# Attention and two MLPs on one core: the MLP's tiles moved to multiples of 512 bytes, and new numbers in the list scheduler

## The chip, the cores and the metric

One core of a Trainium2 chip runs the whole program. The metric is device time in microseconds (us) of one execution. Engines are called as in the profile: PE is TensorE's matmul, PEld its weight load (both are issued by one sequencer), DVE is VectorE, ACT is ScalarE, POOL is GpSimd, SP issues the DMAs.

## What is computed

```
def phi(x):                                   # w_phi: 64 x 128
    proj = x @ w_phi
    proj = proj - max(abs(proj), axis=-1)
    return concat([exp(proj), exp(-proj)])
kv = phi(k).T @ v ; z = sum(phi(k))           # 4 batches, 8 heads, 576 tokens, head 64
attn = (phi(q) @ kv) / (phi(q) @ z + 1e-6)
x = attn                                      # 2304 tokens x 512
h = x @ w_in ; g = where(h > 0, h, exp(min(h, 0)) - 1) ; x = g @ w_out      # MLP 1, 2048 wide
h = x @ w_in2 ; g = h * clip(h + 3, 0, 6) / 6 ; out = g @ w_out2            # MLP 2, 2048 wide
```

The weights of both MLPs arrive as 64-bit floats, everything else in 32 bits.

## The kernel before

**Attention.** Eight units (two heads of two batches each) go through projections, exponentials, the product with v and the normalization. Their result is written into one resident tile `x32` (512 features in four slices of 128 partitions, 2304 tokens).

**MLPs.** Every matmul operand is a pair of fp32r tiles, the rounded value (hi) and the rest (lo), and every product is three matmuls: hi by hi, lo by hi, hi by lo. The hidden width of 2048 is worked in 8 groups of 256 per MLP, `g` from 0 to 15 over both (`NP` = 8). The 2304 tokens are five blocks, four of 512 and one of 256 (block 4). Blocks 0 and 1 are pair `pr` 0, blocks 2 and 3 are pair 1. For a pair, `x @ w_in` of a group is done with seven products P1 to P7 instead of eight (`hid`, L710; Winograd's form of Strassen's scheme), on sums and differences of the quarters: of x they are called A11, A12, A22, S1 to S4, of w_in B11, B21, B12, B22, T1 to T4. Such a product is 6 matmuls of 512 columns. For block 4 it is done directly (`hid4`, L724, twice 12 matmuls of 256 columns). The product with w_out is `outp` (L775): 6 matmuls per block and slice, of 512 columns (256 for block 4 of MLP 1). In a matmul one operand is stationary (loaded by LDWEIGHTS, 128 columns) and one moves. In L710 and L724 w_in is stationary and x moves. In L775 the hidden tile (`ga` or `gb`) moves and w_out is stationary in MLP 1; in MLP 2 it is the other way round.

**Around the matmuls.** The operands of x are made by `x_add` (L687, sums in place), `x_hi` (L693 on ACT, L660 on POOL) and `x_lo` (L696, on DVE for A11, A22, S1, S2 and on POOL for A12, S3, S4). A hidden bank gets its activation by `act1` (ACT, L744 to L747), `gate` (DVE, L751), `gate_hi` (ACT, L755) and `gate_lo` (DVE, L758), and a bank of `x @ w_in` is free again after `gate_lo`; `snap` (ACT, L732) and `join` (DVE, L737) add up the seven products. `sums` (DVE, L787) adds a bank of `outp` to `x32`; three banks serve `outp`, so its next-but-two use waits for that addition. A weight comes by DMA and is turned into fp32 by `low` (ACT), `size` and `end` (POOL, L635 and L651), `sign` and `up` (DVE); then `part_hi` (L664) and `part_lo` (L668) make the hi and lo of w_in, `out_hi` (L673) and `out_lo` (L677) those of w_out. There are 8 w_in tiles, one group's worth, and 3 of w_out.

**Order.** The order of PE's work in the MLPs is written out by hand. Between the MLPs (`g` = 8) it is P1 and P2 of pair 0, the last four `outp` of block 4 of MLP 1 (`kept`), P6, P7, P5, the first `hid4`, P3, P4, the second `hid4`, and then P1 of pair 1. All other engines are ordered by a list scheduler, `in_order`: every step has a duration, the steps that it waits for, and a rank; of the steps of an engine that could start within 0.3 us the one with the lowest rank goes first. The ranks are due times: an operand of x is due `PREP` before its use (16 and 18 us for the two MLPs), the conversions of w_in `W_IN_LEAD` before the group's first product, those of w_out `W_OUT_LEAD` before the first `outp`; steps on hidden banks are due when their product ends. Durations and ranks decide the order in the program alone, not what waits for what.

**Layout.** Tiles are stacked from both ends of a partition's memory. On the left stand `x32`, two small constants, an unused tile `gap`, then `wp` (w_in, w_out), `stg` (staging), and the operands of x but for three; on the right stand, from the end of memory down, S2 and S4 of pair 0, block 4 of x (`x_b4`), `ma`, `mb`, `ga` and `gb`. Each of these tiles is a multiple of 512 bytes, so all tiles of a side share one remainder.

Of the kernel before, what the change touches and what calls it, by code (L numbers as in the profile page):

```python
# [29 lines left out]
}  # L30
KVT = 0.118
W_LEAST, W_MOST = 2.0 ** -15, 122879.9921875
W_IN_LEAD, W_OUT_LEAD = 30.0, 25.0
PREP = (16.0, 18.0)


class Token:
# [111 lines left out]
def attention_then_two_mlps(  # L149
# [67 lines left out]
    nc.gpsimd.memset(half_c, 0.5)  # L217
    two_c = const.tile([128, 1], F32, name="two_c")
    nc.gpsimd.memset(two_c, 2.0)
    const.tile([128, 124], F32, name="gap")  # L220

    wp = ctx.enter_context(tc.tile_pool(name="wp", bufs=1))
    stg = ctx.enter_context(tc.tile_pool(name="stg", bufs=1))
# [586 lines left out]
    def on(engine, us, fn, rank, after):  # L810
        name, us = ("POOL", us[1]) if engine is nc.gpsimd else ("ACT" if engine is nc.scalar else "DVE", us[0])
        return step(name, us, fn, after=after, rank=rank, port=name == "DVE")

    def split(m, pr, op, kk, at, deps, e_hi, e_lo):
        home = last_use[pr, op] if m else [OPEN["b" if pr == 1 else "e" if pr == 0 and op in EARLY else "a"]]
        rank = need[m, pr, op] - PREP[m]
        size = BLOCKS[at[0]][1] / 512
        hi = on(e_hi, (0.05 + 0.52 * size, 0.1 + 0.56 * size), bind_(x_hi, e_hi, pr, op, kk, at), rank, deps + home)
        lo = on(e_lo, (0.1 + 0.6 * size, 0.1 + 1.3 * size), bind_(x_lo, e_lo, pr, op, kk, at), rank, [hi])
        readers.setdefault(at, []).extend([hi, lo])  # L820
        ready.setdefault((m, pr, op), []).append(lo)
        return [hi, lo]
# [89 lines left out]
    def convert(key, lead):  # L912
        m, w, i, c = key
        ts_, ta, tb = Token("s"), Token("ca"), Token(("bi", "bo")[i])
        x = step("SP", 1.4, bind_(fetch, *key), takes=[ts_], rank=lead - 5, behind=[chain[0]] if chain[0] else [])
        chain[0] = x
        low, size, sign, up, end = to_f32(key)
        x = step("ACT", 0.85, low, after=[x], rank=lead, takes=[ta, tb], uses=[ts_])
        z = step("DVE", 0.5, sign, after=[x], rank=lead, port=True, uses=[ts_])
        x = step("POOL", 0.45, size, after=[x], rank=lead)  # L920
        x = step("DVE", 0.3, up, after=[x], rank=lead, port=True)
        return step("POOL", 0.75, end, after=[x, z], rank=lead, uses=[ta, tb]), tb

    for g in range(2 * NP):
        m, w = g // NP, 2 * (g % NP)
        lead = first[g] - W_IN_LEAD
        keys = {"B11": (m, w, 0, 0), "B21": (m, w, 0, 1), "B12": (m, w + 1, 0, 0), "B22": (m, w + 1, 0, 1)}
        done, tok, raw_ = {}, {}, {}

        def part(name, key, after, users):  # L930
            t = wi_tok[g, name] = Token("wi")
            hi = step("ACT", 0.36, bind_(part_hi, g, name, key), after=after, rank=lead, takes=[t], uses=users,
                      behind=[chain[1]] if chain[1] else [])
            chain[1] = hi
            lo = step("POOL", 0.75, bind_(part_lo, g, name, key), after=[hi], rank=lead, uses=users + [t])
# [12 lines left out]
        t3 = differ("B12", "B22", "B12", [done["B12"], raw_["B22"], t1])
        t2 = differ("B22", "B22", "B11", [done["B22"], t1, t3])
        t4 = differ("B21", "B21", "B22", [done["B21"], t2])  # L950
        part("T2", keys["B22"], [t2], [tok["B22"]])
        part("T3", keys["B12"], [t3], [tok["B12"]])
        part("T1", keys["B11"], [t1], [tok["B11"]])
        part("T4", keys["B21"], [t4], [tok["B21"]])
        lead = first_o[g] - W_OUT_LEAD
        for fi in range(2):
            t = wo_tok[g, fi] = Token("wo")
            for c in range(2):
                x, tb = convert((m, w + fi, 1, c), lead)
                hi = step("ACT", 0.36, bind_(out_hi, m, w + fi, c), after=[x] + ([OUT[g, fi]] if c else []),  # L960
                          rank=lead, takes=[] if c else [t], uses=[tb])
                OUT[g, fi] = step("POOL", 0.75, bind_(out_lo, m, w + fi, c), after=[hi], rank=lead, uses=[tb, t])

# [27 lines left out]

    clock = BEGIN
# [7 lines left out]
    for x in order:  # L1000
# [53 lines left out]
        else:  # L1054
# [45 lines left out]
def bind_(fn, *a):  # L1100
    return lambda: fn(*a)
# [50 lines left out]
```

## Time and profile before

| | |
|---|---|
| time, median of 3 runs | 952.58 us (951.78 to 953.23) |
| the profiled execution: its time, its span | 952.91 us, 950.8 us |
| attention, until the first matmul of an MLP | 157.9 us |
| PE busy | 918.8 us, 97% of the span |
| DVE, ACT, POOL busy | 676.0, 566.6, 399.7 us |

The span runs from the first to the last instruction that the profiler saw; the other 2.1 us lie around it. PE is busy nearly all the time, but a matmul's duration in the trace overlaps with the next one, so what a matmul costs PE is the distance from its start to the start of the next.

### The profile page before, as it was taken

To read this page: it belongs to the slowest core of one execution; us is meant where nothing else is said; L and a number is where in the kernel's file an instruction comes from. 1 tells how busy PE (TensorE), PEld (TensorE's weight loads), DVE (VectorE), ACT (ScalarE), POOL (GpSimd) and SP (SyncE) were. 2 spreads that over 40 slices of the span, in tenths; PEclk is the share of its full clock that TensorE was granted. 3 is DMA by queue.
4 is the path that set the end of the run, shared out by engine and by line. 5 is a ranking of instruction groups with operands and counts; after the bars stand their busy time and mean duration, and the time that the engine had idled before them with its cause. 6 is when DMAs were issued, how large, how long until landed. Compare 5 with 4: busy or idle time off the path is not lost.

```text
span 950.8 us, 17635 instructions
## 1 busy us (share of the span) xinstructions
PE 918.8 (97%) x6792; PEld 762.3 (80%) x6792; DVE 676.0 (71%) x1202; ACT 566.6 (60%) x1207; POOL 399.7 (42%) x570
## 2 busy tenths in 40 slices
PE   8999999899999999999999968999999999999998
PEld 7888787688888888888878856888888888888886
DVE  6888877855676767676767797467767676777555
ACT  5686766876665656565666755665545454545331
POOL 0258621453544444444442646545444444444200
PEclk9999999999999999999999987999999999999999
DMA  8534510001111111111111001111111111010013
GB/s 228 160 110 124 147 47 2 1 27 41 45 45 45 45 46 45 45 44 46 45 42 43 29 22 36 43 56 55 46 56 34 57 34 56 33 56 23 1 67 133
DMA packets 42532, 53.69 MB, mean 56 GB/s; under 512 B 21328, under 2 KB 21456, under 8 KB 42448
## 3 DMA queue, kind: packets, MB, share of 16 engines
q1 hardware_dynamic: 42448, 52.57, 17.8%
q8 instruction: 53, 0.87, 0.4%
q14 instruction: 31, 0.25, 0.1%
HBM read 47.84 MB, written 4.72 MB: 55 GB/s over the span
## 4 chain that ended last, share of the span: by engine, by line
PE 88%; DVE 6%; ACT 5%; issue 1%; POOL 0%; POOLq 0%; ACTq 0%
PE ps_a L775 27%; PE ps_p L710 25%; PE ps_t L775 13%; PE ps_t L710 6%; PE ps_t L430 4%; PE ps_a L380 4%; PE ps_p L724 3%; PE ps_p L318 3%; ACT e L407 2%; DVE x L687 1%; DVE x_S L696 1%; PE ps_t L452 1%; PE ps_t L724 1%; DVE x L787 1%; DVE x_A L696 1%
## 5 line engine op out<-in xcount | busy, mean ns | idle before, releaser
L710 PE MATMUL ps_p<-x_S,w_in 128*128 128x512 f32 x630 | 162.6, 397 | 10.0 <-POOL x_S L696 4.1
L787 DVE TENSOR_TENSOR x<-ps_a,x 128x512 f32<-128x512 f32 (+1 forms) x177 | 116.4, 660 | 50.4 <-PE ps_a L775 49.0
L710 PEld LDWEIGHTS ps_p<-x_S,w_in 128*128 128x128 f32 x630 | 118.4, 189 | 39.4 <-POOL x_S L696 4.9
L710 PE MATMUL ps_p<-x_A,w_in 128*128 128x512 f32 x468 | 120.9, 399 | 3.4 <-DVE ga L758 3.4
L668 POOL TENSOR_TENSOR w_in<-w_bi,w_in 128x256 fp32r<-128x256 f32 x128 | 97.7, 782 | 44.7 <-ACT w_in L664 44.2
L635 POOL TENSOR_SCALAR w_a<-w_a 128x256 f32<-128x256 f32 x128 | 53.9, 422 | 146.5 <-ACT w_a L630 146.1
L710 PEld LDWEIGHTS ps_p<-x_A,w_in 128*128 128x128 f32 x468 | 88.5, 191 | 23.3 <-DVE ga L758 4.2
L787 DVE TENSOR_TENSOR x<-ps_t,x 128x512 f32<-128x512 f32 (+1 forms) x89 | 59.0, 663 | 43.0 <-PE ps_t L775 42.6
L651 POOL TENSOR_TENSOR w_bi<-w_bi,w_a 128x256 int32<-128x256 int32 x64 | 47.9, 757 | 95.0 <-DVE w_a L647 95.0
L677 POOL TENSOR_TENSOR w_out<-w_bo,w_out 128x256 fp32r<-128x256 f32 x64 | 48.1, 751 | 94.3 <-ACT w_out L673 93.6
L775 PE MATMUL ps_a<-w_out,gb 128*128 128x512 f32 x336 | 84.9, 395 | 0.0
L775 PE MATMUL ps_a<-gb,w_out 128*128 128x512 f32 (+1 forms) x384 | 83.2, 358 | 0.6 <-DVE x L787 0.6
L651 POOL TENSOR_TENSOR w_bo<-w_bo,w_a 128x256 int32<-128x256 int32 x64 | 48.3, 756 | 65.0 <-DVE w_a L647 62.3
L775 PEld LDWEIGHTS ps_a<-gb,w_out 128*128 128x128 f32 x384 | 64.8, 188 | 13.2 <-DVE x L787 0.8
L775 PEld LDWEIGHTS ps_a<-w_out,gb 128*128 128x128 f32 x336 | 63.0, 188 | 15.1 <-ACT x L785 0.2
L751 DVE SCALAR_TENSOR_TENSOR ps_p<-ma,ps_p 128x512 f32<-128x512 f32 x66 | 45.8, 693 | 30.8 <-ACT ma L747 16.4
L775 PE MATMUL ps_a<-ga,w_out 128*128 128x512 f32 x258 | 65.6, 395 | 0.5 <-DVE ga L758 0.5
L732 ACT COPY mb<-ps_p 128x512 f32<-128x512 f32 x54 | 31.7, 587 | 57.1 <-PE ps_p L710 56.9
L328 DVE TENSOR_REDUCE mx<-ps_p 128x4 f32<-128x512 f32 (+1 forms) x80 | 50.3, 629 | 15.7 <-PE ps_p L318 15.4
L775 PE MATMUL ps_a<-w_out,ga 128*128 128x512 f32 x240 | 60.1, 397 | 0.0
L775 PEld LDWEIGHTS ps_a<-ga,w_out 128*128 128x128 f32 x258 | 47.6, 188 | 11.6 <-DVE ga L758 0.9
L630 ACT ACTIVATE w_a<-w 128x256 f32<-128x256 f32 x128 | 54.3, 424 | 1.1 <-POOL w_bo L651 1.1
(109 smaller groups left out, 1907.1 us busy)
## 6 DMA issues: line engine op xcount, KB each, us to landing
w<-in_moe_w_in_dram SPq DMA_DIRECT2D x64, 256.0 KB, 2.6
w<-in_moe_w_out_dram SPq DMA_DIRECT2D x64, 256.0 KB, 2.6
vb<-in_v_dram SPq DMA_DIRECT2D x16, 288.0 KB, 4.2
out_dram<-x SPq DMA_DIRECT2D x18, 256.0 KB, 2.0
raw_k<-in_k_dram SPq DMA_DIRECT2D x7, 576.0 KB, 4.5
raw_q<-in_q_dram SPq DMA_DIRECT2D x7, 576.0 KB, 4.9
raw_k<-in_k_dram SPq DMA_DIRECT2D x1, 320.0 KB, 4.9
raw_q<-in_q_dram SPq DMA_DIRECT2D x1, 320.0 KB, 5.3
```

Of the source, the lines that this page charges most:

```text
L328: V.tensor_reduce(out=mx[:, :n], in_=P[j, h], axis=AX.X, op=ALU.max, apply_absolute_value=True)
L380: nc.tensor.matmul(out=acc[bb][f0:f0 + 64, h, half], lhsT=kp[p, i, half, f0:f0 + 64], rhs=vb[u % 2][p, r, h], start=(done.count(bb) == 1 a ...
L430: nc.tensor.matmul(out=ps[p, i, h], lhsT=E[h, c][:, half, r - 4 * c, p], rhs=ST[0][:, bb, h, half], start=(half == 0), stop=(half == 1),)
L630: nc.scalar.activation(out=st["a"], in_=s.bitcast(F32).rearrange("p (n t) -> p n t", t=2)[:, :, 1], func=AF.Abs)
L635: nc.gpsimd.tensor_scalar(out=st["a"], in0=st["a"], scalar1=W_MOST, scalar2=W_LEAST, op0=ALU.min, op1=ALU.max)
L651: nc.gpsimd.tensor_tensor(out=b_, in0=b_, in1=st["a"].bitcast(I32), op=ALU.add)
L668: nc.gpsimd.tensor_tensor(out=t[:, 1], in0=F[key], in1=t[:, 0].bitcast(F32), op=ALU.subtract)
L677: nc.gpsimd.tensor_tensor(out=t[:, 1], in0=F.pop((m, w, 1, c)), in1=t[:, 0].bitcast(F32), op=ALU.subtract)
L710: nc.tensor.matmul(out=PS[ps_], lhsT=t[:, a_, kk], rhs=X[pr, op][x_][kk], start=(opens and i == 0), stop=(i == 5), skip_group_check=True,)
L751: V.scalar_tensor_tensor(out=PS[ps_], in0=MAIN[key], scalar=s, in1=PS[ps_], op0=o0, op1=o1)
L775: nc.tensor.matmul(out=o, lhsT=a_, rhs=b_, start=(fi + j == 0), stop=(fi == 1 and j == 2))
L787: V.tensor_tensor(out=part, in0=ps, in1=part, op=ALU.add)
```

## The change

The unused tile `gap` grows from 496 to 832 bytes, and an unused tile of 480 bytes is put at the end of memory on the right. What stands on the left ahead of `gap` ends at byte 38592. Before, `gap` brings that to 39088, which is rounded up to 39104: 192 bytes over a multiple of 512, and so stand all MLP tiles of the left. On the right the stack ended at byte 229344, and all its MLP tiles stand 480 over a multiple. After, the left begins at 38592 + 832 = 39424 and the right ends at 229344 - 480 = 228864, both multiples of 512. In the matmuls of an MLP every slice of a tile begins at a multiple of 512 bytes in its tile, so a remainder holds for every operand: before, both operands stand at 192 in L710 but for S2 and S4 of pair 0 (480 and 192), and one at 480 and one at 192 in L724 and L775; after, all stand at 0.

In the scheduler `W_IN_LEAD` goes from 30 to 15 us, `PREP` of MLP 2 from 18 to 22 us, and the durations of twelve kinds of steps change by up to 12%, that of `act1` in MLP 2 by 21%. No step is added or removed. Line numbers from L221 on are one higher in the changed kernel.

```
-W_IN_LEAD, W_OUT_LEAD = 30.0, 25.0
-PREP = (16.0, 18.0)
+W_IN_LEAD, W_OUT_LEAD = 15.0, 25.0
+PREP = (16.0, 22.0)
...
-    const.tile([128, 124], F32, name="gap")
+    const.tile([128, 208], F32, name="gap")
+    ctx.enter_context(tc.tile_pool(name="gap", bufs=1, side="right")).tile([128, 120], F32, name="gap_r")
...
-        x = step("ACT", 0.57 * (1 + (m == 0)), bind_(act1, m, key, ps_, ring), after=after + [OPEN["a"]], rank=when,
+        x = step("ACT", 1.23 if m == 0 else 0.69, bind_(act1, m, key, ps_, ring), after=after + [OPEN["a"]], rank=when,
```

On PE the order of the MLPs' matmuls is the same word for word; some steps of attention's units 5 to 7 change places. In a group in the middle of an MLP, ACT, DVE and POOL have some conversions a few places later. The largest moves are between the MLPs, where the operands of x for `g` = 8 now rank 4 us earlier.

DVE there, before, from the `x_lo` of S1's first half on (`x32` is written by `x_add` in L687 and by `sums` in L787; gb_6765 is the hidden tile of block 4 that the last four `outp` of MLP 1 read):

```order
L696 TENSOR_TENSOR x_S1_0_119<-x32_63,x_S1_0_119 128x512
L787 TENSOR_TENSOR x32_63<-ps_a1_6733,x32_63 128x512
L696 TENSOR_TENSOR x_S2_0_2919<-x32_63,x_S2_0_2919 128x512
L758 TENSOR_TENSOR gb_6765<-ps_p1_6609,gb_6765 128x512
L687 TENSOR_TENSOR x32_63<-x32_63 128x512
L696 TENSOR_TENSOR x_A22_0_118<-x32_63,x_A22_0_118 128x512
L787 TENSOR_TENSOR x32_63<-ps_t0_6747,x32_63 128x512
```

The same place after, where gb_6776 is that hidden tile and the first row is the second row behind the first `x_lo` of S2:

```order
L697 TENSOR_TENSOR x_A22_0_122<-x32_63,x_A22_0_122 128x512
L788 TENSOR_TENSOR x32_63<-ps_t0_6700,x32_63 128x512
L688 TENSOR_TENSOR x32_63<-x32_63 128x512
L788 TENSOR_TENSOR x32_63<-ps_a0_6712,x32_63 128x512
L688 TENSOR_TENSOR x32_63<-x32_63 128x512
L788 TENSOR_TENSOR x32_63<-ps_a1_6723,x32_63 128x512
L688 TENSOR_TENSOR x32_63<-x32_63 128x512
L697 TENSOR_TENSOR x_S1_0_123<-x32_63,x_S1_0_123 128x512
L788 TENSOR_TENSOR x32_63<-ps_t0_6735,x32_63 128x512
L697 TENSOR_TENSOR x_S2_0_2923<-x32_63,x_S2_0_2923 128x512
L688 TENSOR_TENSOR x32_63<-x32_63 128x512
L759 TENSOR_TENSOR gb_6776<-ps_p1_6611,gb_6776 128x512
```

The `gate_lo` stood right behind the first `x_lo` of S2 and now stands 13 places behind it, behind the second halves of A22, S1 and S2 too. Ahead of it nine steps are new and three (of a weight's conversion) are gone.

POOL between the MLPs, before (w_out_6831 is the second w_out tile of `g` = 8):

```order
L651 TENSOR_TENSOR w_bo_6579<-w_bo_6579,w_a_6578 128x256
L696 TENSOR_TENSOR x_S3_0_120<-x32_63,x_S3_0_120 128x512
L677 TENSOR_TENSOR w_out_6831<-w_bo_6579,w_out_6831 128x256
L651 TENSOR_TENSOR w_bo_6642<-w_bo_6642,w_a_6641 128x256
L677 TENSOR_TENSOR w_out_6831<-w_bo_6642,w_out_6831 128x256
L696 TENSOR_TENSOR x_S4_0_2920<-x32_63,x_S4_0_2920 128x512 x2
```

and after:

```order
L697 TENSOR_TENSOR x_S3_0_124<-x32_63,x_S3_0_124 128x512
L669 TENSOR_TENSOR w_in_6753<-w_bi_6354,w_in_6753 128x256
L669 TENSOR_TENSOR w_in_6765<-w_bi_6328,w_in_6765 128x256
L669 TENSOR_TENSOR w_in_6768<-w_bi_6252,w_in_6768 128x256
L669 TENSOR_TENSOR w_in_6774<-w_bi_6277,w_in_6774 128x256
L697 TENSOR_TENSOR x_S4_0_2924<-x32_63,x_S4_0_2924 128x512 x2
L678 TENSOR_TENSOR w_out_6542<-w_bo_6480,w_out_6542 128x256
```

The two `x_lo` of S4 stood behind an `end` and the last `out_lo` of the second w_out tile, and now stand ahead of both.

ACT between the MLPs, before, after the `gate_hi` of P5 and P7's bank (ma_6939 and ga_6958 are `act1` and `gate_hi` of P3's bank):

```order
L693 CAST x_S3_1_3111<-x32_63 128x512
L693 CAST x_S2_1_3110<-x32_63 128x512
L693 CAST x_S1_1_3112<-x32_63 128x512
L747 ACTIVATE ma_6939<-ps_p2_6758,half_c_69 128x512
L693 CAST x_S3_1_3111<-x32_63 128x512
L755 CAST ga_6958<-ps_p2_6758 128x512
```

and after, where ma_6930 and ga_6941 are those two, ma_6937 is `act1` of the second `hid4`, gb_6925 is `gate_hi` of a bank that `join` made with P7, and mb_6853 is `act1` of the bank of P7 and P4:

```order
L756 CAST gb_6925<-ps_p1_6886 128x512
L748 ACTIVATE ma_6930<-ps_p2_6745,half_c_69 128x512
L694 CAST x_S3_1_3115<-x32_63 128x512
L748 ACTIVATE ma_6937<-ps_p0_6872,half_c_69 128x512
L756 CAST ga_6941<-ps_p2_6745 128x512
L748 ACTIVATE mb_6853<-ps_t1_6844,half_c_69 128x512
```

The `act1` of P3's bank is now ahead of the `x_hi` of S1 and S2 for pair 1, and its `gate_hi` has the `act1` of the second `hid4` ahead of it.

## Rows read from the trace of the kernel before

**Rows 1.** The page: span, and busy time, share and instructions.

```profile
span 950.8 us, 17635 instructions
PE 918.8 (97%) x6792; PEld 762.3 (80%) x6792; DVE 676.0 (71%) x1202; ACT 566.6 (60%) x1207; POOL 399.7 (42%) x570
```

**Rows 2.** PE's timeline in MLP 1: start, length, line, tiles, count.

```profile
360.29 1.56 PE L775 MATMUL ps_t<-gb,w_out 128*128 128x512 f32 x6
361.69 1.56 PE L710 MATMUL ps_p<-x_S,w_in 128*128 128x512 f32 x6
363.09 2.96 PE L775 MATMUL ps_a<-gb,w_out 128*128 128x512 f32 x12
365.89 1.55 PE L710 MATMUL ps_p<-x_S,w_in 128*128 128x512 f32 x6
367.27 1.52 PE L710 MATMUL ps_t<-x_S,w_in 128*128 128x512 f32 x6
368.63 1.52 PE L710 MATMUL ps_p<-x_A,w_in 128*128 128x512 f32 x6
369.99 1.56 PE L710 MATMUL ps_p<-x_S,w_in 128*128 128x512 f32 x6
```

**Rows 3.** PE's timeline in MLP 2.

```profile
749.54 1.56 PE L724 MATMUL ps_p<-x_b,w_in 128*128 128x256 f32 x12
750.94 2.96 PE L775 MATMUL ps_a<-w_out,ga 128*128 128x512 f32 x12
753.74 1.56 PE L775 MATMUL ps_t<-w_out,ga 128*128 128x512 f32 x6
```

**Rows 4.** Matmuls (PE) and loads of L710, L724, L775, in this order, over both MLPs.

```profile
150.00:951.00 801.00, 340.86 (x1344) 254.67 (x1344) 0.99 0.13 43
150.00:951.00 801.00, 51.02 (x384) 49.57 (x384) 0.99 0.13 43
150.00:951.00 801.00, 431.24 (x1824) 329.07 (x1824) 0.99 0.13 43
```

**Rows 5.** Two stretches: length; PE, PEld, DVE, ACT, POOL busy; granted clock; DMA.

```profile
300.00:350.00 50.00, 50.00 (x245) 41.55 (x245) 35.32 (x64) 30.84 (x66) 21.10 (x33) 1.00 0.13 43
555.00:560.00 5.00, 3.14 (x7) 2.33 (x8) 5.00 (x12) 2.60 (x7) 2.70 (x2) 0.72 0.00 0
```

**Rows 6.** PE's timeline between the MLPs; in brackets idle time and what ended it.

```profile
552.29 0.97 PE L775 MATMUL ps_a<-gb,w_out 128*128 128x256 f32 x6 [0.56 <-DVE x L787]
...
555.72 0.50 PE L710 MATMUL ps_p<-x_S,w_in 128*128 128x512 f32 x1 [1.76 <-ACT x_S L693]
557.36 1.22 PE L710 MATMUL ps_p<-x_S,w_in 128*128 128x512 f32 x2 [1.14 <-DVE x_S L696]
...
568.07 2.64 PE L710 MATMUL ps_p<-x_S,w_in 128*128 128x512 f32 x5 [4.08 <-POOL x_S L696]
570.51 2.76 PE L710 MATMUL ps_t<-x_A,w_in 128*128 128x512 f32 x6
573.07 2.13 PE L724 MATMUL ps_p<-x_b,w_in 128*128 128x256 f32 x12
578.59 5.49 PE L710 MATMUL ps_p<-x_A,w_in 128*128 128x512 f32 x12 [3.39 <-DVE ga L758]
```

**Rows 7.** DVE's timeline between the MLPs.

```profile
546.80 1.18 DVE L696 TENSOR_TENSOR x_S<-x,x_S 128x512 fp32r<-128x512 f32 x1
547.91 0.68 DVE L758 TENSOR_TENSOR gb<-ps_p,gb 128x512 fp32r<-128x512 f32 x1
```

**Rows 8.** POOL's timeline between the MLPs.

```profile
565.34 1.01 POOL L677 TENSOR_TENSOR w_out<-w_bo,w_out 128x256 fp32r<-128x256 f32 x1 [4.17 <-ACT w_out L673]
566.31 3.12 POOL L696 TENSOR_TENSOR x_S<-x,x_S 128x512 fp32r<-128x512 f32 x2
```

**Rows 9.** ACT's timeline between the MLPs.

```profile
574.20 0.62 ACT L693 CAST x_S<-x 128x512 fp32r<-128x512 f32 x1 [6.66 <-DVE x L687]
574.73 0.68 ACT L747 ACTIVATE ma<-ps_p,half_c 128x512 f32<-128x512 f32 x1
576.17 0.59 ACT L755 CAST ga<-ps_p 128x512 fp32r<-128x512 f32 x1 [0.26 <-DVE ps_p L751]
```

More of the change, by code (lines that the diff above doesn't have):

```diff
@@ L817, in split @@
         size = BLOCKS[at[0]][1] / 512
-        hi = on(e_hi, (0.05 + 0.52 * size, 0.1 + 0.56 * size), bind_(x_hi, e_hi, pr, op, kk, at), rank, deps + home)
+        hi = on(e_hi, (0.05 + 0.55 * size, 0.1 + 0.56 * size), bind_(x_hi, e_hi, pr, op, kk, at), rank, deps + home)
         lo = on(e_lo, (0.1 + 0.6 * size, 0.1 + 1.3 * size), bind_(x_lo, e_lo, pr, op, kk, at), rank, [hi])
@@ L917, in convert @@
         low, size, sign, up, end = to_f32(key)
-        x = step("ACT", 0.85, low, after=[x], rank=lead, takes=[ta, tb], uses=[ts_])
-        z = step("DVE", 0.5, sign, after=[x], rank=lead, port=True, uses=[ts_])
+        x = step("ACT", 0.95, low, after=[x], rank=lead, takes=[ta, tb], uses=[ts_])
+        z = step("DVE", 0.45, sign, after=[x], rank=lead, port=True, uses=[ts_])
         x = step("POOL", 0.45, size, after=[x], rank=lead)
@@ L931, in part @@
             t = wi_tok[g, name] = Token("wi")
-            hi = step("ACT", 0.36, bind_(part_hi, g, name, key), after=after, rank=lead, takes=[t], uses=users,
+            hi = step("ACT", 0.40, bind_(part_hi, g, name, key), after=after, rank=lead, takes=[t], uses=users,
                       behind=[chain[1]] if chain[1] else [])
@@ L959, in attention_then_two_mlps @@
                 x, tb = convert((m, w + fi, 1, c), lead)
-                hi = step("ACT", 0.36, bind_(out_hi, m, w + fi, c), after=[x] + ([OUT[g, fi]] if c else []),
+                hi = step("ACT", 0.40, bind_(out_hi, m, w + fi, c), after=[x] + ([OUT[g, fi]] if c else []),
                           rank=lead, takes=[] if c else [t], uses=[tb])
@@ L971, in finish @@
         pt, mt = ptok[ps_], mtok[key]
-        x = step("ACT", 0.57 * (1 + (m == 0)), bind_(act1, m, key, ps_, ring), after=after + [OPEN["a"]], rank=when,
+        x = step("ACT", 1.23 if m == 0 else 0.69, bind_(act1, m, key, ps_, ring), after=after + [OPEN["a"]], rank=when,
                  takes=[mt] if ring else [], uses=[pt, mt])
-        x = step("DVE", 0.64, bind_(gate, m, key, ps_), after=[x], rank=when, uses=[pt, mt])
-        x = step("ACT", 0.57, bind_(gate_hi, key, ps_, tg.ring), after=[x], rank=when, takes=[tg], uses=[tg, pt],
+        x = step("DVE", 0.69, bind_(gate, m, key, ps_), after=[x], rank=when, uses=[pt, mt])
+        x = step("ACT", 0.58, bind_(gate_hi, key, ps_, tg.ring), after=[x], rank=when, takes=[tg], uses=[tg, pt],
                  behind=[gg_last[tg.ring]] if tg.ring in gg_last else [])
         gg_last[tg.ring] = x
-        tiles[key] = step("DVE", 0.65, bind_(gate_lo, key, ps_), after=[x], rank=when, uses=[tg, pt])
+        tiles[key] = step("DVE", 0.685, bind_(gate_lo, key, ps_), after=[x], rank=when, uses=[tg, pt])
     def save(g, pr, key, ring, after, when):
         t = mtok[key] = Token(ring)
-        return step("ACT", 0.57, bind_(snap, (g, pr, "X"), key, ring), after=after, rank=when, takes=[t],
+        return step("ACT", 0.59, bind_(snap, (g, pr, "X"), key, ring), after=after, rank=when, takes=[t],
                     uses=[ptok[g, pr, "X"], t])
@@ L988, in joined @@
             ptok[g, pr, to] = Token("h")
-        return step("DVE", 0.65, bind_(join, (g, pr, bank_), key, (g, pr, to)), after=after, rank=when,
+        return step("DVE", 0.70, bind_(join, (g, pr, bank_), key, (g, pr, to)), after=after, rank=when,
                     takes=[ptok[g, pr, to]] if to != bank_ else [], uses=[pt, ptok[g, pr, to], mtok[key]])
@@ L1074, in attention_then_two_mlps @@
             else:
-                y = step("DVE", 0.65 if m or b < 4 else 0.38, bind_(sums, m, False, b, d), after=[s, adds[m, b, d]], rank=when, uses=[ty])
+                y = step("DVE", 0.66 if m or b < 4 else 0.41, bind_(sums, m, False, b, d), after=[s, adds[m, b, d]], rank=when, uses=[ty])
             adds[m, b, d] = y
```

## The prediction

> **What bounds the kernel now.** I read the page first: PE is busy 918.8 of 950.8 us [rows 1]. That is no proof that matmuls set the time, so I looked at stretches: in the middle of MLP 1 PE is busy 50.00 of 50 us at clock 1.00, and DVE, ACT and POOL 35, 31 and 21 us [rows 5]. No other engine is near its limit there, and PE's timeline shows no wait; the reader is to see in [rows 2] that each group of six follows the one before at once. So the time of the MLPs is a sum of distances from one matmul's start to the next one's, and busy times don't give them, since durations overlap: a group of six has a length of 1.52 to 1.56 us but starts 1.36 to 1.40 us before the next.
>
> These distances are not all alike. With one operand at remainder 480 and the other at 192, six matmuls of 512 columns take 1.40 us: 361.69 to 363.09 in L710 (by PE's order the S2 of pair 0), and in L775 two groups from 363.09 to 365.89 [rows 2]; it is the same in MLP 2, where w_out moves: twelve in 2.80 [rows 3]. With both at 192 they take 367.27 to 368.63 = 1.36 us, and again 1.36, and 1.38 (365.89 to 367.27) where the group ahead was a mixed one [rows 2]. Shape, type and line (L710) are the same; I found no other difference than the addresses. Twelve of 256 columns with mixed remainders take 749.54 to 750.94 = 1.40 [rows 3]. One matmul of 512 is thus 233.3 ns mixed and 226.7 ns equal. At the lower clock six take 570.51 to 573.07 = 2.56 us, 427 ns each [rows 6]; half of it, 213.3 ns, is what 512 columns would take at the higher clock (2.4 instead of 1.2 GHz) without any excess. The excess now is 20 ns or 13.3 ns.
>
> The one place where PE waits long is between the MLPs, 545 to 590 us. Its waits there are 0.56, 1.76, 1.14, 4.08 and 3.39 us, 10.9 in all [rows 6]. Matmuls behind them run at the lower clock for a while; from the groups' distances there, against those of [rows 2], I work out a loss of some 7.9 us in three stretches of 1.9, 3.1 and 3.0 us.
>
> **The addresses.** 3552 matmuls belong to the MLPs [rows 4]. L710 has 1344; of these S2 and S4 of pair 0 are mixed, 2 products x 16 groups x 6 = 192, and 1152 are equal. L775 has 1824, of which block 4 in MLP 1 (8 groups x 4 slices x 6 = 192) has 256 columns, so 1632 have 512. L724 has 384 of 256 columns. All are mixed in L724 and L775. After, every operand stands at 0, so both are equal. No row shows two operands at 0. From above the price is bounded by the mixed 1.40 us, from below by the excess-free 1.28; the nearest row is that of two equal remainders, 1.36, which I take.
>
> - Mixed, 512 columns: 1632 + 192 = 1824, 304 groups of six, each 1.40 - 1.36 = 0.04 shorter: 12.2 us.
> - Equal, 512 columns: 192 groups. In PE's order 126 of them follow a mixed one and lose 0.02 by it: 2.5 us.
> - 256 columns: 384 + 192 = 576, 48 groups of twelve, 0.04 each if the excess falls in the same ratio: 1.9 us.
>
> Together 16.6 us. About 3% of the matmuls lie between the MLPs, where waits or the lower clock decide, so 16 us stay. This rests on PE alone: none of it is covered by other work, since PE waits for nothing, and the other engines keep a margin (DVE 35.32 of 50 [rows 5]); with six in 1.36 a group of the hidden width is 2% shorter, which they can follow.
>
> The Trainium skill ("TensorE: Matmul & The Clock Gate", section "Back-to-back issue gap") gives N/2.4 GHz and some 2.5 ns from start to start, 215.7 ns for 512 columns, whatever the addresses. The rows have 226.7 and 233.3, so the rule does not describe this kernel as it is; if it did after the change, the address term would be about 52 instead of 16.6, by its figure an estimate. The case has its place among the rivals.
>
> **The scheduler in the middle of an MLP.** `W_IN_LEAD` and the durations move some conversions a few places on ACT, DVE and POOL. No instruction is added; a w_in tile is still loaded and converted a group ahead, since the ring has one group's worth, and PE waits nowhere in these stretches. I price it at 0. The cover is PE's own work in a group, some 47 us; what is left idle on the fullest engine, DVE, is 14.7 of 50 us [rows 5]. If the cover failed, the price would be one wait per group of a conversion's length, about 1 us (an `out_lo` took 1.01 [rows 8]) x 16 = 16 us. Attention's units 5 to 7 change places without a change of work: 0, I allow 2 us either way.
>
> **Between the MLPs.** POOL first. PE waits 4.08 us for the `x_lo` of S4 [rows 6], which POOL starts at 566.31, behind an `out_lo` that itself waited 4.17 us for ACT [rows 8]. After, both `x_lo` of S4 stand ahead of it. POOL would have been free before that wait, so S4 comes at least 3 us earlier, and with it P3: 4.08 us goes, together with most of one stretch at the lower clock (3 us).
>
> DVE next. It is full there (5.00 of 5.00 us, while the clock is 0.72 [rows 5]), so an order can only shift the loss. The `gate_lo` of block 4 ran at 547.91 right behind an `x_lo` [rows 7]; now nine steps are new ahead of it and three gone. Nine at 0.68 are 6.1 us, less some 1.4 for the three and 1.25 that DVE idled ahead: about 3.5 us later, so it ends at 552.1 instead of 548.6. The last four `outp` of MLP 1 want it at about 549.2: a new wait of 2.9 us. Queued behind it on PE are P6, P7 and P5. But the second halves of S1 and S2 stand ahead of that `gate_lo` now, so the waits of 1.76 and 1.14 us for S2 [rows 6] go, as does most of the 0.56: 3.4 against 2.9. The next thing to be late would be the `sums` of these `outp` and behind them block 4's operand, which the first `hid4` reads.
>
> ACT last. The 3.39 us ahead of P1 of pair 1 [rows 6] ends with the `gate_lo` of P3's bank. ACT had waited 6.66 us at an `x_hi` with the bank's `act1` queued behind it [rows 9]. After, that `act1` goes ahead, but the `gate_hi` stands behind the `act1` of the second `hid4`, which PE finishes last: `act1`, `gate_hi` and `gate_lo` of 0.68 + 0.59 + 0.68 and some 0.25 of handing over come after it, 2.2 us instead of 3.39: 1.2 saved. Operands of pair 1 that are late on DVE can cost 1.5 to 5 us a little later; I take 3.
>
> Sum: -4.1 - 3.0 - 3.4 + 2.9 - 1.2 + 3 = -5.8, say -6 us. Bounds: all waits and all loss of the clock gone, -10.9 - 7.9 = -19; nothing gone and both new waits added, 2.9 + 3.3 = +6.
>
> **Sum.** The profiled execution took 952.91 us (950.8 and 2.1 around it [rows 1]), 0.3 above the median of the runs. 952.9 - 16 - 6 = 930.9; I say 930 us for the median.
>
> **Rivals.**
>
> *The excess goes away altogether* (0.18). The excess grows with columns and changes with the remainder, so it may come from starting off a boundary, and a multiple of 512 could leave little of it. For: 192 and 480 are both off 512, and no row shows an operand that is on it. Against: one remainder of 192 and one of 480 differ by a third of the excess only. At 1.28 us per group: 304 x 0.12 + 126 x 0.10 + 66 x 0.08 + 48 x 0.12 = 60 us, 58 without the middle: 889 us. Halfway to the equal rows, 1.32, gives some 909. The figure of the skill above would give about 897, an estimate.
>
> *Addresses don't matter* (0.20). The difference could belong to something that goes with the remainder, such as which pools are read, and the change moves all of them. Then the schedule alone remains: 952.9 - 6 = 947 us. Against it: the S2 at 361.69 and the S3 at 367.27 are one line with weights from one pool and differ in nothing else. The Trainium skill ("SBUF — State Buffer", section "Who interferes with whom") says that PE never waits on anyone and has ports of its own for the moving operand and for the weight load; by that the 1.36 and 1.40 of [rows 2] should be one number, and they are not.
>
> *Zero is a bad remainder* (0.08), and the kernel gets slower. Two operands on the same multiple may collide at every start. The groups now sum to 304 x 1.40 + 126 x 1.38 + 66 x 1.36 + 48 x 1.40 = 756 us over 544 groups, 1.391 each; with 6 us from the schedule it decides from 1.402 per group on. One more step of 0.04 above the mixed ones, 1.44, would cost 544 x 0.05 = 27 us: 974 us. Against: of the rows, equal is the faster.
>
> *Schedule and addresses cancel* (0.04): 1.39 per group and +2 between the MLPs, 953 to 955 us.
>
> **Numbers.** The forecast, six in 1.36 everywhere, has 0.50, and its own range from the bounds between the MLPs and in attention is 920 to 941. The range over all, 895 to 949, reaches to most of the case without excess and to the schedule alone, and leaves out the slower ones and the lowest end. A measurement of this kernel can tell about 0.2% (1.9 us) from no change; by that, faster 0.86, same 0.05, slower 0.09.
>
> **What would show it.** Right: every group of six, L710 or L775, in both MLPs starts 1.36 us ahead of the next, twelve of 256 columns in 1.36; no wait of 4.08 us for S4 on POOL; a new wait for `gb` at about 549 us less what the matmuls have gained by then. Wrong in size: groups of 1.28 to 1.34. Wrong in kind: groups still of two lengths, or at 1.40 and more; waits of PE in the middle of an MLP for w_in or for a bank; or a sum of waits between the MLPs above 11 us.

## The result and the profile after

The changed kernel takes 938.29 us, the median of 4 runs (937.94 to 938.99), against 952.9 us (951.78 to 953.49) for the kernel before in the same session: a ratio of 0.9849, 95% interval 0.9832 to 0.9866, or 14.6 us less. The forecast was 930 us, some 22 us less, and the case of the forecast, six matmuls in 1.36 us, is the one that came. The page of the changed kernel, which answers to [rows 1]:

```profile
span 937.2 us, 17621 instructions
PE 903.2 (96%) x6792; PEld 759.3 (81%) x6792; DVE 677.9 (72%) x1202; ACT 567.3 (61%) x1207; POOL 398.0 (42%) x570
```

PE's busy time fell by 15.6 us and the span by 13.6; the other engines' work hardly moved. PE's timeline at the place in MLP 1 that [rows 2] shows of before (start, length, line, tiles, count):

```profile
356.89 1.52 PE L776 MATMUL ps_a<-gb,w_out 128*128 128x512 f32 x6
358.25 1.52 PE L776 MATMUL ps_t<-gb,w_out 128*128 128x512 f32 x6
359.61 1.52 PE L711 MATMUL ps_p<-x_S,w_in 128*128 128x512 f32 x6
360.97 2.88 PE L776 MATMUL ps_a<-gb,w_out 128*128 128x512 f32 x12
363.69 1.52 PE L711 MATMUL ps_p<-x_S,w_in 128*128 128x512 f32 x6
```

From start to start: 1.36 us for each six, L711 and L776 alike, 2.72 for the twelve. The same in MLP 2 at a block 4, beside [rows 3]:

```profile
735.63 1.69 PE L725 MATMUL ps_p<-x_b,w_in 128*128 128x256 f32 x12
737.16 1.55 PE L776 MATMUL ps_t<-w_out,ga 128*128 128x512 f32 x6
738.54 1.60 PE L725 MATMUL ps_p<-x_b,w_in 128*128 128x256 f32 x12
739.98 2.91 PE L776 MATMUL ps_a<-w_out,ga 128*128 128x512 f32 x12
742.72 1.52 PE L776 MATMUL ps_t<-w_out,ga 128*128 128x512 f32 x6
744.08 1.52 PE L711 MATMUL ps_t<-x_A,w_in 128*128 128x512 f32 x6
```

Here two things differ from the forecast. Twelve of 256 columns take 738.54 to 739.98 = 1.44 us, more than the 1.40 of before and not less. And a group of 512 columns behind them takes 1.38 (737.16 to 738.54), the one after that 1.36.

Between the MLPs, PE's timeline with its waits (in brackets), to be held against [rows 6]:

```profile
538.14 3.01 PE L776 MATMUL ps_a<-gb,w_out 128*128 128x512 f32 x12 [0.81 <-DVE x L788]
541.85 1.65 PE L776 MATMUL ps_t<-gb,w_out 128*128 128x512 f32 x6 [0.69 <-DVE x L788]
...
549.48 1.46 PE L776 MATMUL ps_a<-gb,w_out 128*128 128x256 f32 x10 [2.70 <-DVE gb L759]
...
554.87 1.58 PE L776 MATMUL ps_a<-gb,w_out 128*128 128x256 f32 x6 [3.21 <-DVE x L788]
...
569.15 3.03 PE L711 MATMUL ps_p<-x_A,w_in 128*128 128x512 f32 x12 [1.98 <-DVE ga L759]
...
573.49 0.73 PE L776 MATMUL ps_a<-w_out,ga 128*128 128x512 f32 x2 [0.40 <-POOL w_out L678]
...
578.49 1.65 PE L776 MATMUL ps_a<-w_out,ga 128*128 128x512 f32 x6 [1.53 <-ACT x L786]
...
581.64 0.73 PE L711 MATMUL ps_p<-x_S,w_in 128*128 128x512 f32 x2 [0.60 <-DVE x_S L697]
```

The waits of 1.76, 1.14 and 4.08 us of before are gone, the 3.39 is 1.98, and the forecast wait for `gb` stands at 549.48 with 2.70. But a wait of 3.21 for `sums` follows it, two of 0.81 and 0.69 for `sums` stand ahead, and three come later: 11.9 us in all, where before had 10.9. What was gained is the clock: only one stretch is left in which PE was granted less than full clock, 555 to 560:

```profile
545.00:555.00 10.00, 4.03 (x25) 3.08 (x24) 10.00 (x12) 3.85 (x8) 10.00 (x9) 1.00 0.08 26
555.00:560.00 5.00, 5.00 (x18) 4.23 (x19) 4.13 (x10) 3.28 (x9) 1.40 (x2) 0.66 0.00 0
560.00:600.00 40.00, 35.50 (x175) 29.11 (x174) 31.73 (x48) 28.41 (x60) 23.47 (x28) 1.00 0.13 40
```

(Length; PE, PEld, DVE, ACT, POOL busy; granted clock; DMA.) DVE and POOL were busy for every one of the 10 us in which PE stood still for more than half, 545 to 555. DVE's timeline there:

```profile
548.75 0.68 DVE L759 TENSOR_TENSOR gb<-ps_p,gb 128x512 fp32r<-128x512 f32 x1
...
550.43 3.45 DVE L697 TENSOR_TENSOR x_A<-x,x_A 128x512 fp32r<-128x512 f32 x2
553.81 0.69 DVE L738 TENSOR_TENSOR ps_p<-ps_p,ma 128x512 f32<-128x512 f32 x1
554.41 0.74 DVE L788 TENSOR_TENSOR x<-ps_a,x 128x256 f32<-128x256 f32 x2
```

The `gate_lo` comes at 548.75, and then two `x_lo` of pair 1, which PE wants only at 569, ahead of the `sums` that frees the bank for the last `outp`. They take 1.7 us each, where others of this shape take 0.68, and run beside two `x_lo` of POOL:

```profile
550.32 3.02 POOL L697 TENSOR_TENSOR x_S<-x,x_S 128x512 fp32r<-128x512 f32 x2
```

### The profile page after: what moved, and what is told of

Read it like the earlier page. It is cut to its first block, busy times and chain, and to the rows that moved or that the text cites. A ratio compares the mean times of both kernels' runs of the same rounds, so it can differ in the third digit from the quotient of the medians.

```text
span 937.2 us, 17621 instructions
## 1 busy us (share of the span) xinstructions
PE 903.2 (96%) x6792; PEld 759.3 (81%) x6792; DVE 677.9 (72%) x1202; ACT 567.3 (61%) x1207; POOL 398.0 (42%) x570
## 4 chain that ended last, share of the span: by engine, by line
PE 88%; DVE 7%; ACT 4%; issue 1%; POOL 0%; POOLq 0%; ACTq 0%
PE ps_a L776 26%; PE ps_p L711 25%; PE ps_t L776 13%; PE ps_t L711 6%; PE ps_p L725 4%; PE ps_a L381 4%; PE ps_t L431 4%; PE ps_p L319 3%; ACT e L408 2%; DVE x L688 2%; DVE x_S L697 1%; PE ps_t L453 1%; PE ps_t L725 1%; DVE x_A L697 1%; DVE x L788 1%
## 5 line engine op out<-in xcount | busy, mean ns | idle before, releaser
L711 PE MATMUL ps_p<-x_S,w_in 128*128 128x512 f32 x630 | 159.3, 392 | 4.3 <-ACT mb L733 2.1
L711 PEld LDWEIGHTS ps_p<-x_S,w_in 128*128 128x128 f32 x630 | 118.5, 189 | 30.4 <-ACT mb L733 2.7
L669 POOL TENSOR_TENSOR w_in<-w_bi,w_in 128x256 fp32r<-128x256 f32 x128 | 94.8, 758 | 88.7 <-ACT w_in L665 88.5
L711 PE MATMUL ps_p<-x_A,w_in 128*128 128x512 f32 x468 | 117.4, 391 | 2.0 <-DVE ga L759 2.0
L711 PEld LDWEIGHTS ps_p<-x_A,w_in 128*128 128x128 f32 x468 | 86.9, 188 | 20.1 <-DVE ga L759 2.6
L776 PE MATMUL ps_a<-gb,w_out 128*128 128x512 f32 (+1 forms) x384 | 82.8, 357 | 6.8 <-DVE x L788 4.0
L776 PE MATMUL ps_a<-w_out,gb 128*128 128x512 f32 x336 | 82.7, 389 | 0.0
L776 PEld LDWEIGHTS ps_a<-gb,w_out 128*128 128x128 f32 x384 | 65.6, 191 | 18.7 <-DVE x L788 4.6
L776 PEld LDWEIGHTS ps_a<-w_out,gb 128*128 128x128 f32 x336 | 63.1, 188 | 13.1
L776 PE MATMUL ps_a<-ga,w_out 128*128 128x512 f32 x258 | 64.3, 391 | 0.5 <-DVE ga L759 0.5
L776 PE MATMUL ps_a<-w_out,ga 128*128 128x512 f32 x240 | 59.1, 391 | 1.9 <-ACT x L786 1.5
L776 PEld LDWEIGHTS ps_a<-ga,w_out 128*128 128x128 f32 x258 | 47.7, 188 | 10.4 <-DVE ga L759 0.9
```

The costliest lines, as they stand in the source:

```text
L669: nc.gpsimd.tensor_tensor(out=t[:, 1], in0=F[key], in1=t[:, 0].bitcast(F32), op=ALU.subtract)
L711: nc.tensor.matmul(out=PS[ps_], lhsT=t[:, a_, kk], rhs=X[pr, op][x_][kk], start=(opens and i == 0), stop=(i == 5), skip_group_check=True,)
L776: nc.tensor.matmul(out=o, lhsT=a_, rhs=b_, start=(fi + j == 0), stop=(fi == 1 and j == 2))
```

## The experiments

**The two parts apart.** One kernel has the addresses of after and the scheduler's numbers of before, another the reverse.

```
 e1:                                        e2:
 W_IN_LEAD = 30, PREP = (16, 18)            W_IN_LEAD = 15, PREP = (16, 22)
 durations of before                        durations of after
 gap 208 words, gap_r 120 words             gap 124 words, no gap_r
```

> The addresses alone, with the order of before. Theory: in the traces of before and after the matmuls of the MLPs, waits and the lower clock left out, take 233.3 against 227.2 ns in L775 and 230 against 227.2 in L710 with 512 columns, and 117 against 119.5 with 256; over 1632, 1344 and 576 that is -9.9, -3.7 and +1.4, about -12, of which the part at the lower clock gets nothing: 941 to 942 us. Rival: the faster matmuls reach the place between the MLPs earlier, DVE is full there, and part is waited away again: 945 us, with waits between the MLPs of 13 us and more where before had 10.9.

> The scheduler's numbers alone, with the addresses of before. Theory: between the MLPs the wait for S4 (4.08 us) and two of three stretches at the lower clock go, and new waits of about 2.7 for the hidden tile of block 4 and 3.2 for sums stand there: 4 to 5 us off, 948 to 949 us; every group of six keeps its 1.36 or 1.40. Rival: the order only pays with the faster matmuls, or costs in the middle of the MLPs: 952 to 954 us.

The addresses alone: 941.23 us, ratio 0.9881 (0.9866 to 0.9895), 11.4 us less, as expected; the waits between the MLPs sum to 12.4 us, a little more than before, so some of the rival is in it. The schedule alone: 951.07 us, ratio 0.9971 (0.9954 to 0.9989), 1.6 us less. That is less than expected, and its 9 runs lie between 947.45 and 952.42, while those of the addresses alone lie within 0.6 us; the profiled one, at 951.09, had a stretch at lower clock at the start of MLP 1 that the profile of after lacks. The four of the nine runs with a mean granted clock of 0.998, which all runs of after have, took 947.45 to 950.22, the five below it 951.07 to 952.42. So 1.6 us is a middle over both, and the expected 4 to 5 us are near what the first have, 2.4 to 5.2. By the medians the two parts make 13.0 of the 14.6 us.

**Which addresses.** The next two keep the order of before and move only the unused tiles: left and right at remainders 192 and 448, and at 32 and 32. Each kernel of this part ran once; the twelve runs of the kernel before beside these two took 951.65 to 956.42 us.

```
 e3: gap 124 words (as before), gap_r   8 words      192 and 448
 e4: gap  88 words,             gap_r 112 words       32 and  32
```

> The order of before, left tiles at 192 as before, right tiles at 448 instead of 480 over a multiple of 512. Theory of the difference (what counts is that both operands share a remainder of 512): groups of six in L775 stay at 1.40 us and the time at 952.5. Rival, theory of 64 bytes (an operand that starts off a multiple of 64 costs): 448 and 192 are both multiples of 64, so all groups of six are at 1.36, twelve of 256 columns at 1.44, and the time is that of the addresses alone, 941 to 942.

> The order of before, left and right tiles both at 32 over a multiple of 512. Theory of the difference: equal remainders, so groups of six at 1.36 us, twelve of 256 columns at 1.44, 941 to 942 us. Rival, theory of 64 bytes: both operands start off a multiple of 64, so groups of six are at 1.40 or more, in L710 too, and the time is 955 us or more.

Each theory lost one. With 192 and 448, 939.98 us, against the theory of the difference; with 32 and 32, 940.93 us, against that of 64 bytes. PE's timeline of the first, in MLP 1:

```profile
356.78 1.52 PE L776 MATMUL ps_a<-gb,w_out 128*128 128x512 f32 x6
358.14 1.52 PE L776 MATMUL ps_t<-gb,w_out 128*128 128x512 f32 x6
359.50 1.52 PE L711 MATMUL ps_p<-x_S,w_in 128*128 128x512 f32 x6
360.86 2.88 PE L776 MATMUL ps_a<-gb,w_out 128*128 128x512 f32 x12
```

And of the second, with both at 32:

```profile
357.38 1.52 PE L776 MATMUL ps_t<-gb,w_out 128*128 128x512 f32 x6
358.74 1.52 PE L711 MATMUL ps_p<-x_S,w_in 128*128 128x512 f32 x6
360.10 2.88 PE L776 MATMUL ps_a<-gb,w_out 128*128 128x512 f32 x12
```

All groups of six in these rows are at 1.36 us. What the fast layouts have in common is a difference of 0 or 256 between the two operands; the slow one of before has 288. So a multiple of 512, which the change aims at, is not what counts, and neither is standing at a multiple of 64. Which differences are slow, the next two ask.

```
 # e5, order of before, left and right at 0; 32 bytes behind each tile of x, ga, gb
-t = pool_.tile([128, 2, 2, 512], F32R, ...)
+t = pool_.tile([128, 2056], F32R, ...)[:, :2048].rearrange(...)
 # e12, order of before: left at 0, right at 128
 gap 208 words, gap_r 88 words
```

> The order of before, weights at remainder 0, and 32 bytes of padding behind every operand of x and every hidden tile, so that each stands at another remainder: x of pair 0 at 0, 32, 64, 96, 128 and (S2, S4) 288, 320, x of pair 1 at 160 to 352 in steps of 32, block 4 at 352, ga at 384 and 416, gb at 448 and 480. Theory of 64: only the difference of the two operands modulo 64 counts, so groups with 32, 96, 160, 224, 288, 352, 416, 480 take 1.40 us and those with 0, 64, 128, 192, 256, 320, 384, 448 take 1.36. Rival, theory of 256: only differences of 0 and 256 are fast, and 64, 128, 192, 320, 384 and 448 take 1.40 too, or a step between.

> The order of before, left tiles at 0, right tiles at 128 over a multiple of 512, so that L775, L725 and S2 and S4 of pair 0 have a difference of 128 and all else of 0, with no third remainder beside them. Theory of 256 (only differences of 0 and 256 are fast): groups of six in L776 at 1.39 to 1.40 us, some 951 to 953 us. Rival, theory of 64 or 128 (a multiple of that is enough, and the kernel with steps of 32 was slow because a group at another remainder slows the one behind it): all groups at 1.36, 941 us.

With steps of 32 bytes the kernel takes 956.07 us, slower than before. PE's timeline in MLP 1:

```profile
360.89 1.55 PE L776 MATMUL ps_a<-gb,w_out 128*128 128x512 f32 x6
362.28 1.55 PE L776 MATMUL ps_t<-gb,w_out 128*128 128x512 f32 x6
363.67 1.56 PE L711 MATMUL ps_p<-x_S,w_in 128*128 128x512 f32 x6
365.07 2.93 PE L776 MATMUL ps_a<-gb,w_out 128*128 128x512 f32 x12
367.84 1.56 PE L711 MATMUL ps_p<-x_S,w_in 128*128 128x512 f32 x6
369.24 1.56 PE L711 MATMUL ps_t<-x_S,w_in 128*128 128x512 f32 x6
370.64 0.63 PE L711 MATMUL ps_p<-x_A,w_in 128*128 128x512 f32 x2
```

Groups of six take 1.39 twice (`gb`), 1.40 (S2, 288), half of 2.77 (`gb` again), 1.40 (S1, 96) and 1.40 (S3, 128). A group with `gb` reads both tiles of that name, three matmuls at a difference of 448 and three at 480, so it tests neither; S3 is a clean one, and the theory of 64 expected 1.36 for it. But each group stands behind one at another remainder here, and that alone costs something, as [rows 2] has it; a lone group at difference 0 or 256 wasn't at 1.36 either in this kernel. Over the whole kernel the products of one difference average 1.38 to 1.395 us at the multiples of 64 and 1.399 to 1.405 at the others, a step that the theory of 256 doesn't explain. Hence the clean case with a difference of 128 and no third remainder: 952.78 us, beside 952.79 of the kernel before. Its PE timeline:

```profile
361.76 1.56 PE L711 MATMUL ps_p<-x_S,w_in 128*128 128x512 f32 x6
363.16 2.96 PE L776 MATMUL ps_a<-gb,w_out 128*128 128x512 f32 x12
365.96 1.54 PE L711 MATMUL ps_p<-x_S,w_in 128*128 128x512 f32 x6
367.33 1.52 PE L711 MATMUL ps_t<-x_S,w_in 128*128 128x512 f32 x6
368.69 1.52 PE L711 MATMUL ps_p<-x_A,w_in 128*128 128x512 f32 x6
```

S2 at a difference of 128 takes 1.40, `gb` 1.40 each, S1 at 0 behind them 1.37, S3 at 0 behind S1 1.36. The theory of 256 holds in all five layouts with one or two remainders: 288 and 128 are slow, 0 and 256 fast, wherever the pair itself stands. No other difference was run without a third remainder beside it.

**Which of the scheduler's numbers.** With the addresses of after throughout, the three edits (W_IN_LEAD 30 or 15, PREP of MLP 2 18 or 22, durations old or new) are taken apart; first the kernel after with one edit undone at a time:

```
 e6: after, PREP = (16.0, 18.0)     e7: after, W_IN_LEAD = 30.0     e8: after, durations of before
```

> The kernel after with PREP of MLP 2 back at 18. The order between the MLPs is then much that of before (the gate_lo of block 4 stands behind the first x_lo of S2 again, the x_lo of S4 behind the out_lo). Theory: PREP carries what the scheduler's numbers bring, so the wait for S4 is back with 3 to 4 us and the time is that of the addresses alone, 941 us. Rival: W_IN_LEAD or the durations carry it: 938 to 939 us.

> The kernel after with W_IN_LEAD back at 30. The order between the MLPs on DVE is nearly that of after. Theory (PREP carries it): 938 to 939 us, and the waits of 0.2 to 0.3 us for the bank at the first hid4 of a group of MLP 2, which after has and the order of before has not, are gone, which is about 1 us. Rival: W_IN_LEAD carries it: 941 us.

> The kernel after with the durations of before. Theory (PREP carries it): 938 to 939 us, no wait for S4. Rival: the durations carry it: 941 us.

My theory, that PREP carries the gain, fell, and with it the rivals as I had put them: without PREP's edit the kernel is faster still, 936.46 us (0.9825, 0.9808 to 0.9842), and without either of the others slower than the addresses alone, 946.78 (0.9936, 0.9919 to 0.9952) and 946.14 (0.9926, 0.9902 to 0.9950). Of e7's small waits at the first `hid4` in MLP 2 I had expected that they go; they are there, in five groups. So I formed another, that the durations carry it, and made the two single edits, and PREP in between:

```
 e9:  e1 with W_IN_LEAD = 15.0
 e10: e1 with the durations of after
 e11: after, PREP = (16.0, 20.0)
```

> The addresses and W_IN_LEAD 15; PREP 18 and the durations of before. POOL's order between the MLPs is that of before: the x_lo of S4 stands behind the last out_lo. Theory (the durations bring the gain, the lead does not): the wait of about 4 us for S4 stays, from the first matmul of the MLPs to the last 777 to 778 us as with the addresses alone, 941 us. Rival (the lead brings it): 772 to 773 us, 936 to 937 us.

> The addresses and the new durations; PREP 18 and W_IN_LEAD 30. The first x_lo of S4 stands ahead of the last out_lo on POOL. Theory (the durations bring the gain): from the first matmul of the MLPs to the last 772 to 774 us, no wait of 4 us for S4, 936 to 938 us. Rival (the lead brings it): 777 to 778 us, 941 us.

> The kernel after with PREP of MLP 2 at 20. If the loss from 18 to 22 is the place of the gate_lo of block 4, it comes with its place: its wait of 2.7 us is there or not, and the time is near 938 with it and near 936.5 without. Rival: a smooth loss, 937.4 us.

This fell too. The lead alone gives 940.39 (0.9877, 0.9862 to 0.9891), the durations alone 950.55 (0.9974, 0.9963 to 0.9984), and PREP 20 takes 940.68 (0.9881, 0.9864 to 0.9897), more than 18 and 22, which is neither of the two expectations. All kernels with the addresses of after, from each one's own profile; the last two columns run from the first matmul of `g` = 7 to that of `g` = 9, and from there to the end of the span. The profiled execution of e10 took 947.59 us, 3.0 less than its median, that of e6 935.44, 1.0 less.

| kernel | lead, PREP, durations | median us | first matmul of an MLP at | from there to the end of the span | waits of PE listed from 535 to 600 | `g` = 7 and 8 | `g` = 9 on |
|---|---|---|---|---|---|---|---|
| e1 | 30, 18, old | 941.23 | 157.5 | 781.4 | 12.4 | 113.2 | 339.9 |
| e9 | 15, 18, old | 940.39 | 159.4 | 779.1 | 8.3 | 107.7 | 340.3 |
| e10 | 30, 18, new | 950.55 | 160.1 | 785.2 | 13.8 | 113.6 | 341.6 |
| e6 | 15, 18, new | 936.46 | 157.6 | 775.9 | 8.6 | 106.1 | 341.6 |
| e11 | 15, 20, new | 940.68 | 158.3 | 780.8 | 10.7 | 111.2 | 341.4 |
| after | 15, 22, new | 938.29 | 158.2 | 779.0 | 11.9 | 109.4 | 341.4 |
| e7 | 30, 22, new | 946.78 | 162.3 | 781.7 | 11.1 | 110.4 | 341.3 |
| e8 | 15, 22, old | 946.14 | 161.5 | 783.5 | 12.5 | 113.5 | 340.4 |

In the whole time no number has a worth of its own: new durations cost 9.3 us with a lead of 30 (e1 to e10) and bring 3.9 with a lead of 15 (e9 to e6). Part of it lies in attention, up to the first matmul of an MLP, where the kernels differ by up to 4.8 us, and part in which waits the new order happens to make between the MLPs. e7 and e8 are slower than e1 mostly by attention: 4.8 of some 5.5 us and 4.0 of 4.9.

By stretches the numbers come apart better. Over `g` = 7 and 8 the lead alone (e9) already saves 5.5 us of the 7.1 that lead and durations save together (e6), and the durations alone (e10) save nothing. e9 loses its gain again ahead of that, 1.9 us in attention and 3.1 in the first group of MLP 1, where PE waits for an `x_hi` of pair 1; e8, with the same lead and durations, has that wait too (2.09), and in e6 it is 0.29:

```profile
192.84 0.50 PE L711 MATMUL ps_p<-x_S,w_in 128*128 128x512 f32 x1 [2.08 <-ACT x_S L694]
```

The new durations cost 1.4 to 1.7 us from `g` = 9 on in every kernel that has them, against 0.5 at most in e8 and e9. A PREP of 20 or 22 brings the wait for `gb` and those of about 0.7 to 1.2 us for `sums` ahead of it, which no kernel with 18 has, and takes away that for S4.

In the durations alone, the first of these two rows of PE is the largest single wait of all kernels:

```profile
585.40 0.80 PE L711 MATMUL ps_p<-x_S,w_in 128*128 128x512 f32 x1 [6.97 <-ACT x_S L694]
588.09 1.22 PE L711 MATMUL ps_p<-x_S,w_in 128*128 128x512 f32 x2 [1.90 <-DVE x_S L697]
```

And in e6, the fastest kernel of the study, the longest waits are these two (of nine, 8.6 us in all), with neither the wait for `gb` nor the 3.21 behind it:

```profile
559.41 0.97 PE L711 MATMUL ps_p<-x_S,w_in 128*128 128x512 f32 x3 [2.15 <-POOL x_S L697]
...
568.69 3.02 PE L711 MATMUL ps_p<-x_A,w_in 128*128 128x512 f32 x12 [2.56 <-DVE ga L759]
```

## Why the prediction was right, and where its sizes were off

**The address term was right in kind and 4.6 us too large.** 16 us were predicted and 11.4 measured by the addresses alone. The 512-column steps came as worked out: every group, mixed or equal before, is at 1.36 us. PE's order in the MLPs is the same in the kernel before and e1, so their matmuls can be compared one by one, those behind a wait or at the lower clock left out: the mixed ones of 512 columns give 10.7 us, where 12.2 were predicted, the equal ones 2.5 as predicted, and those of 256 columns cost 1.3, where 1.9 were to be gained. The step that failed is the third, "0.04 each if the excess falls in the same ratio" for 256 columns: one of them went from 117.1 to 119.4 ns from start to start, and the term is 3.2 us off. A smaller miss is a group of 512 behind one of 256, at 1.38 to 1.39 instead of 1.36; 44 such places in PE's order are about 1.1 us. 16.6 - 3.2 - 1.1 less the share between the MLPs, 0.6 in the prediction, leaves 11.7.

**The rivals on the addresses.** That they don't matter is refuted most simply by e3 and e12, where only the size of two unused tiles differs and the time differs by 12.8 us. The Trainium skill ("SBUF — State Buffer", section "Who interferes with whom") has PE waiting on nobody; the rows at 1.36 and 1.40 of one line in one kernel (e12) speak against reading that as independence of where PE's own two operands lie. That the excess goes away did not happen: no group of six went below 1.36. By the Trainium skill's N/2.4 GHz and 2.5 ns ("TensorE: Matmul & The Clock Gate", section "Back-to-back issue gap") six would take 1.29, an estimate, which no run here shows. The section gives that formula for an isolated matmul, and for a stream with weight loads some 131 ns at 512 columns; the rows at 226.7 ns agree with neither. That zero is a bad remainder is refuted by the result; that zero is a good one, by e4, since 32 and 32 does as well.

**The schedule's 6 us were 2.9** (941.23 to 938.29). By the profiles of e1 and after it saves 3.8 us over `g` = 7 and 8, of which some 1.4 are lost from `g` = 9 on and 0.7 in attention. Between the MLPs, step by step:

- The wait for S4 goes: right. The wait for S2 (1.76 and 1.14) goes: right.
- The new wait for `gb`: 2.9 predicted, 2.70 measured, in its place.
- The 3.39 falls to 2.2: it fell to 1.98.
- Operands of pair 1 late, taken as 3: 0.40 + 1.53 + 0.60 = 2.5, though only the last is an operand of x.
- "As does most of the 0.56": wrong. What stood there as 0.56 became 3.21. I followed the queue behind the `gate_lo` on PE, but on DVE only up to the `gate_lo`; behind it stand two `x_lo` of A11 for pair 1, 3.45 us, and then the `sums`. That is the failed step, 2.7 us.
- The 0.81 and 0.69 ahead weren't seen: with the operands of x ranked 4 us earlier, DVE makes them before the `sums` of pair 1's last banks, too. 1.5 us.
- One stretch at the lower clock was to go (3 us); two went. Counted over single matmuls (those 427 or 214 ns from the next, less 227 or 120), the loss fell from 5.9 us (32 matmuls) to 1.4 (9), so 4.5; the 7.9 of the prediction was too high.

The measured items sum to -4.1 - 2.9 + 2.7 - 1.4 + 2.5 + 2.7 + 1.5 - 4.5 = -3.5 us, where -5.8 was forecast. Beside e1, whose waits sum to 12.4 us, nearly all of what is saved there is clock: the waits of after are 0.5 us less.

In MLP 2 the forecast of 0 missed 1.4 us: PE's first `hid4` starts 0.2 us late in five groups and loses another 0.1 behind its first matmul, which neither before nor e1 has. The new durations bring it, as the last column of the table shows.

The forecast's own range of 920 to 941 us is narrower than its bounds give: 952.9 - 16 - 19 - 2 = 916 to 952.9 - 16 + 6 + 2 = 945. The measured time lies in both.

**The attribution was wrong though the sign was right.** For e6 I put the gain between the MLPs down to the earlier operands of x (PREP 22). e6 shows the opposite: with the other edits in place, 22 costs 1.8 us against 18 by the medians, 3.1 by the two profiles from the first matmul of an MLP on (779.0 and 775.9). The gain is the other two edits' together (e1 to e6, 4.8 us), and in the whole time neither has it alone. Between the MLPs it is the lead's, 5.5 of 7.1 us, and the new durations spare the lead its loss in the first group of MLP 1. Why the lead gives a better order there isn't settled by these runs: the table shows that the waits change, and not a rule by which; nor is it shown how much of the difference in attention belongs to the order.

## What to carry to other kernels

Read what a matmul costs from start to start, and group it by where the operands lie as well as by shape: two unused tiles were worth 11 us here, and other sizes do as well (e3, e4). When a scheduler's numbers are changed, measure them in combination, and stretch by stretch; a row of single changes, by the whole time alone, would have rejected the pair that gains. When a step is moved back in a queue, follow the queue beyond that step, to whatever the waiting engine needs next.

## What the runs showed of the hardware that was not expected

- At the higher clock, a matmul of 512 fp32r columns takes 226.7 ns from start to start when its two operands differ by 0 or 256 bytes modulo 512, and about 233 when they differ by 128 or 288; the place itself doesn't matter (0 and 0, 32 and 32, 192 and 448 all fast). Other differences were only tried mixed together, at 1.37 to 1.41 for six. What in the chip does it isn't shown.
- The excess of the fast kind is the same for both lengths: 226.7 is 13.3 ns above 213.3, half of what it takes at the lower clock, and the 120 of most 256-column matmuls is 13.3 above 106.7, half of that. At a difference of 288 the excess goes with the columns: 20 and 10 ns. So of these two the better layout is the worse one for 256 columns. At a difference of 128 it is not so: there the 256-column ones take 119 on average, as in the fast layouts.
- The start of a program can differ where the order of PE doesn't. In e7 and e8 PE ran at a lower clock from 10 to 14 us; of e7 the windows (columns as above):

```profile
8.00:10.00 2.00, 0.49 (x4) 0.36 (x4) 1.97 (x4) 1.30 (x3) 0.00 (x0) 1.00 1.16 229
10.00:12.00 2.00, 2.00 (x16) 1.78 (x17) 1.79 (x3) 1.00 (x2) 0.00 (x0) 0.60 1.02 378
12.00:14.00 2.00, 2.00 (x33) 1.67 (x32) 1.88 (x3) 1.32 (x3) 0.00 (x0) 0.55 1.07 303
```

The kernel after has a granted clock of 1.00 there. PE's order is the same in both up to that place, but already the first 16 matmuls of attention take longer, 4.96 to 6.83 in e7 and 4.96 to 6.17 in after:

```profile
4.96 2.08 PE L319 MATMUL ps_p<-wphi,raw_k 64*128 64x128 f32 x16
6.83 1.13 PE L319 MATMUL ps_p<-wphi,raw_q 64*128 64x128 f32 x16
```

In the traces' records of the clock the first stretch at the higher level begins at 7.0 us in e7 and 6.6 in e8, at 5.4 in after and at 4.2 to 6.1 in the others. By 16 us e7 is 1.8 us behind after (16.08 and 14.32 for the same 16 matmuls of L319). e7 and e8 reach the MLPs 3 to 4 us later than after; the rest comes later, and from 19 us on PE's orders differ. That is one profiled execution of each. The four times of each kernel agree within 3 us, but whether their starts were alike isn't recorded, and what sets the start isn't shown.
